# Funnel attention followed by a multiplicative feed-forward: constants through TensorE at the start, another early order, and later key and query transposes on SyncE

## The chip, the cores and the metric

The kernel runs on one core of a Trainium2 chip. The metric is the device time of one execution in microseconds. The kernel before was run three times. A separate execution was profiled; its trace is what is read below. The engines are called as in the profile: PE is TensorE (PEld its weight loads), DVE is VectorE, ACT is ScalarE, POOL is GpSimd, SP is SyncE, which here only issues DMAs.

## What is computed

Eight batches of eight heads, 1152 positions, 64 features a head. Queries are averaged in pairs, which leaves 576 rows a head; after attention, the heads of a batch stand side by side as 512 features of 4608 tokens, which go through two gates, a product, and two more matrices.

```python
def _attn_ref(q, k, v):
    q_pool = q.reshape(B, H, S // 2, 2, D).mean(axis=3)
    scores = scale * np.matmul(q_pool, k.transpose(0, 1, 3, 2))
    scores = scores - np.max(scores, axis=-1, keepdims=True)
    attn = np.exp(scores)
    attn = attn / (np.sum(attn, axis=-1, keepdims=True) + 1e-09)
    return np.matmul(attn, v)

def _moe_ref(x, w1, w2, w3, w_out):
    a = x @ w1
    b = x @ w2
    h = a * b @ w3
    return (h @ w_out)
```

Inputs and output are float32; the kernel works in float16 with float32 sums, and leaves the maximum out of the softmax.

## The kernel before

**Pairs and chunks.** Two heads of one batch form a pair P (0 to 31); head u of the pair uses the partitions 64u to 64u+63 of the transposed keys `kT[P]` and pooled queries `qT[P]`. The transposed scores of a pair are 9 key blocks of 128 by 576 queries, 5184 columns for each head. They are cut, across the pairs, into 324 chunks of 512 columns; a pair is 10.125 chunks. `scores(c)` (matmuls at L287) writes a chunk of both heads into one of two PSUM tiles `psc`, `expo(c)` (L293) takes its exponential on ScalarE into a ring `er`. `attend(P, u)` multiplies the exponentials by the values with a column of ones: 36 matmuls at L305, and for u = 0 18 more at L314 for the last 64 query rows of both heads. `normalize` divides on VectorE (L333, L336, L347), and SyncE transposes the result by DMA into `xT` (L341) or, for the last rows, `xR` (L323).

**Feed-forward.** w3 and w_out are multiplied with each other first: w3 is transposed on TensorE (`w3t`, L458), copied (L449), multiplied by w_out (`pT`, L470) and kept as `T16`. When the four pairs of a batch have ended, `add_batch` queues its gates (`pg`, L506: 256 tokens by w1 and by w2 for each of 8 blocks of 128 and each of two parities h; then VectorE L490 and L498 form `gT`) and its rows (`pp`, L527, stored through SyncE). Every fourth batch brings a second unit for the remainder rows in `xR`, 128 wide. Most of these matmuls contract over 64 partitions, one half of the array each: there is a queue for each half, and products of the two halves lie side by side in time.

**Keys and queries.** For pairs 0 to 8 they are transposed on TensorE (`prep_first`, `prep_rest`; `prep_stage` stages, and `prep_pe` transposes, L255). From pair 9 on `prep_dma` does it: POOL rearranges the keys (`kc`, L159), pools the queries (`qp`, L143) and copies the values (L152); SyncE transposes keys (L160) and queries (L162) by DMA; then POOL reads one element of `kT` (`seen`, L166) and issues the loads of pair P + 5, so those start only when the key transpose has landed.

**The order.** No scheduler orders the instructions. The kernel's own loop writes them out by a planner: two clocks, one for each half of the array, are advanced by booked costs (0.219 for the scores of a chunk, 0.216 for a 512-wide half product, and so on), `due(c)` says when the scores of a chunk may come, `step(h)` takes the next product from the queues `prep` and `ffn` if its data are ready by the clock, `bursts` holds the attends. What comes early is tied to the place of the chunk in pairs: `STAGE` and `PREP` (pairs), `early` (chunk and block of w3), `events` (loads, and `copy_v`). Small VectorE work waits in `jobs`, one a chunk. PSUM has two `psc` tiles and four banks `ff0` to `ff3`, which `spare` hands out; a new tile in a bank has to wait for the old one.

**Queues.** All loads go through POOL in the order written: q and k of pair 0, v of pair 0, k and q of pair 1, the first quarter of w3, w_out whole (`load_w`), then pair 2 and so on. SyncE's queue holds the transposes and the stores in the order written; an entry whose data are not ready holds those behind it.

Of the kernel before, what the change touches and what calls it, by code (L numbers as in the profile page):

```python
# [8 lines left out]
FP16 = mybir.dt.float16  # L9
# [14 lines left out]
def kernel(  # L24
# [20 lines left out]
    NPE = 9  # L45
    T_SC, T_EXP, T_SEM, T_PV, LEAD = 0.219, 1.03, 0.25, (1.65, 1.3), 2.6
    SCALE = 0.5 * float(D) ** -0.5

# [22 lines left out]
    ctx.enter_context(tc.manual_schedule())  # L71

    for vt in vts:
        nc.vector.memset(vt[:, :, :, D:VW], 1.0 / SCL)
# [6 lines left out]
    exp_done = []  # L81
    spare = [(0.0, n) for n in range(4)]

    def vector(n, at):

        nonlocal vec
        vec = max(vec, at + T_SEM) + 0.16 + n / 960
        return vec

    def bank(pre, n, dt=FP32):  # L90
        if n >= 4:
            return psum.tile([128, 2, 512], FP32, tag="psc", bufs=2, name=pre)[:, 0, :]
        return psum.tile([128, 2048 // (4 if dt == FP32 else 2)], dt, tag=f"ff{n}", bufs=1,
                         name=pre)

    def take():
# [30 lines left out]
    def load(P):  # L127


        if P < NP:  # L130
            load_k(P)
            load_q(P)
        if P <= NP:
            load_v(P - 1)
# [16 lines left out]
    def copy_v(P, eng=None):  # L151
        (eng or nc.vector).tensor_copy(out=vts[P % 4][:, :, :, 0:D], in_=vst.pop(P))  # L152

    def prep_dma(P):

        pp, o = P // 2, 64 * (P % 2)
        new_kq(P)
        kc = ab.tile([128, NJ, 2, D], FP16, tag="kc", bufs=2, name="kc")
        nc.gpsimd.tensor_copy(out=kc.rearrange("p j u d -> p u j d"), in_=kst.pop(P))  # L159
        nc.sync.dma_start_transpose(out=kT[P], in_=kc.rearrange("p j u d -> p (j u d)"))  # L160
        pool_q(P, nc.gpsimd)
        nc.sync.dma_start_transpose(  # L162
            out=qT[P], in_=qps[pp][o:o + 64].rearrange("p c u d -> p (c u d)"))
        copy_v(P, nc.gpsimd)
        if P + 5 <= NP:
            nc.gpsimd.tensor_copy(out=seen[:, 0:1], in_=kT[P][0:1, 0, 0:1])  # L166
            load(P + 5)

# [52 lines left out]
    def prep_rest(tb):  # L221
        nc.vector.tensor_copy(out=kcs[0][:, 3:NJ].rearrange("p j u d -> p u j d"),
                              in_=kst[0][:, :, 3:NJ])
        keys(0, tb, range(3, NJ))
        nc.vector.tensor_copy(out=kT[0][:, 3:NJ].rearrange("p j f -> p (j f)"),
                              in_=tb[:, 0:768])
        copy_v(0)
        del kst[0], kcs[0]
# [133 lines left out]

    def load_w(dst, src):
        nc.gpsimd.dma_start(out=dst, in_=src.rearrange("(c p) f -> p c f", p=128))

# [35 lines left out]

    w3T = {}

    class Block:
# [36 lines left out]
    def w3_transpose(c):  # L441

        w3T[c] = ffp.tile([128, NF, 128], FP16, tag="w3T", bufs=4, name="w3T")
        ready = [1e9]
        left = [2]
        landed = 13.0

        def out(t, at, h):
            nc.vector.tensor_copy(out=w3T[c][:, :, 64 * h:64 * h + 64],  # L449
                                  in_=t[:, 0:512].rearrange("p (a f) -> p a f", f=64))  # L450
            done = vector(256, at)
            left[0] -= 1
            if left[0] == 0:
                ready[0] = max(done + T_SEM, landed)
            return done

        def emit(t, s, n, start, stop):
            nc.tensor.transpose(t[:, 64 * n:64 * n + 64],  # L458
                                w3h[c // 2][s, c % 2, 128 * n:128 * n + 128], ident[s, s])
        for h in range(2):  # L460
            add(prep, Block("w3t", NF, (h,), lambda t, at, h=h: out(t, at, h), FP16),
                0.0285, [[0.0]], emit)

        def copy(t, at):
            nc.vector.tensor_copy(out=T16[:, c, :], in_=t)
            del w3T[c]
            return vector(512, at)

        def product(t, s, n, start, stop):
            nc.tensor.matmul(t, w3T[c][s, n, :], wosb[s, n, :], start=start, stop=stop,  # L470
                             skip_group_check=True)
        add(ffn, Block("pT", NF, (0, 1), copy), 0.216, [ready], product)

    def add_unit(n, x, places, ready, final=False):

# [6 lines left out]
        def gate(ft, h):  # L482
            def mul(t, at):
# [8 lines left out]
                if h not in gT:  # L492
                    gT[h] = ffp.tile([128, NF, 256], FP16, tag="g", bufs=4, name="gT")
                g = gT[h][:, ft, 0:n]
# [39 lines left out]

        for h in range(2):
            for ft in range(NF):
                gate(ft, h)
        for h, o, to in places:
            rows(h, o, to)

    def add_batch(b, ready):

        k, o, end = (b // 2) % 2, 256 * (b % 2), b == B - 1
        add_unit(256, lambda s, m: xT[s, m, k, o:o + 256],
                 [(h, 128 * i, [(b, 4 * i + 2 * h), (b, 4 * i + 2 * h + 1)])
                  for h in range(2) for i in range(2)], ready)
        if b % 4 == 3:
            add_unit(128, lambda s, m: xR[s, m // 2, b // 2 - 1:b // 2 + 1, m % 2],
                     [(h, 0, [(b - 3 + h, 8), (b - 1 + h, 8)]) for h in range(2)],
                     ready, final=end)  # L550

# [35 lines left out]
    def last_rows(places, lhsT):  # L587
# [25 lines left out]
        base=0, channel_multiplier=1, pattern=[[-1, 128]])  # L613
    load_v(0)
    load_k(1)
    load_q(1)
    load_w3(0)
    load_w(wosb, moe_w_out)
    load(2)
# [4 lines left out]
    nc.gpsimd.tensor_copy(out=swap[:, 64:128], in_=ident[:, 0:64])  # L624
    staged, prepped = 1, 1
    rest = prep_first()

    def last_chunk(P):
        return -(-(P + 1) * PAIR // CH) - 1

    def copy_v_later(P):
        if P < 4:
            jobs.append((560, lambda: copy_v(P)))
        else:
            copy_v(P, nc.gpsimd)

    early = [(14, 0), (14, 1), (19, 2), (20, 3), (26, 4), (27, 5), (33, 6), (34, 7)]
    STAGE = {1: 0.39, 2: 1.4, 3: 2.15, 4: 2.85, 5: 3.85}
    PREP = {1: 0.55, 2: 1.6, 3: 2.45, 4: 3.2, 5: 4.1}
    events = sorted(  # L640
        [(0.0, 4, load), (0.0, 3, load_w3), (0.4, 5, load), (0.4, 0, load_ffn), (1.2, 6, load),
         (1.2, 1, load_ffn), (2.3, 7, load), (4.0, 8, load), (4.75, 9, load), (5.0, 10, load),
         (5.95, 11, load), (6.95, 12, load), (7.05, 13, load)]
        + list(zip((1.75, 2.6, 3.7, 4.35, 5.1, 5.4, 6.1, 7.0), range(1, NPE),
                   [copy_v_later] * NPE)), key=lambda e: e[0])
    WEIGHTS = (47.0, 57.0)
    jobs = []
    kq_done[0] = 0.0
    bursts = sorted([(last_chunk(P) + (2 if u == 1 else 6), P, u)
                     for P in range(NP) for u in range(2)])  # L650

    def due(c):


        if bursts and (c + 1) * CH > bursts[0][1] * PAIR + RING:
            return 1e9
        P = ((c + 1) * CH - 1) // PAIR
        return max(exp_done[c - 2] if c > 1 else 0.0, kq_done.get(P, 0.0))

    c = 0  # L660
    fresh = False
    while c < NCHUNK or bursts or ffn[0] or ffn[1]:
        h = 0 if clock[0] <= clock[1] else 1
        if bursts and (c > bursts[0][0] or c == NCHUNK) and spare and spare[0][0] < clock[h] and (
                fresh or c > bursts[0][0] + 1 or c == NCHUNK):
            attend(*bursts.pop(0)[1:])
            fresh = False
            while swap_due():
                swap_halves()
            continue  # L670
        if c >= NCHUNK or due(c) > clock[h]:
# [5 lines left out]
            if not step(h):  # L677
                if swap_due():
                    clock[:] = [max(clock) + 0.1] * 2
                    swap_halves()  # L680
                    clock[:] = [clock[0] + 0.1] * 2
                else:
                    clock[h] += 0.02
# [9 lines left out]
        expo(c)  # L693
        exp_done.append(max(exp_done[-1] if c else 0.0, max(clock) + T_SEM) + T_EXP)
        if c == 0:
            prep_rest(rest)
        if jobs:
            n, job = jobs.pop(0)
            job()
            vector(n, 0.0)  # L700
        if staged < NPE and at >= STAGE.get(
                staged, staged - (0.95 if staged < 4 else 1.3)):
            prep_stage(staged)
            staged += 1
        while events and at >= events[0][0]:
            _, n, act = events.pop(0)
            act(n)
        todo = prepped < NP and at >= PREP.get(prepped, prepped - (
            0.65 if prepped < 4 else 0.9 if prepped < NPE else 1.9))
        if todo and prepped >= NPE:  # L710
            prep_dma(prepped)
            prepped += 1
        elif todo and prepped < staged and prepped in kcs:
            prep_pe(prepped)
            prepped += 1
        elif early and c >= early[0][0] and len(w3T) < 4:
            w3_transpose(early.pop(0)[1])
        c += 1
# [37 lines left out]
```

## Time and profile before

| what | value |
|---|---|
| median of 3 runs | 424.46 us (422.82 to 424.8) |
| the profiled execution | 422.81 us |
| its span, first to last instruction | 420.7 us |
| first scores on PE, first exponential on ACT | 8.05 us, 8.70 us |
| last exponential | starts at 367.4 us |
| ACT exponentials (L293) | 324, 308.2 us, 1029 ns each |
| waits of POOL's `seen` for the key transpose | 83.6 us in 19 |
| key transpose, issue to landing (median of 23) | 7.4 us |
| xT transpose, issue to landing (median of 64) | 4.7 us |

Times in the trace count from the first instruction of the program, L12 is line 12 of the kernel before. Group lines read: line, engine, operation, out<-in, shape, count, then busy time and mean ns of one, then the idle time of the engine just before them and what ended it. Busy matmuls overlap, so a busy TensorE need not be at its peak: its two halves may be filled by one product alone. The granted clock (PEclk) is what the throttle allowed, as a share of full speed.

### The profile page before, as it was taken

The page shows a single profiled execution, that of the slowest core. Times are in us where ns is not written, and L with a number is a line of the kernel's source. Part 1 is how long each engine was busy: PE and PEld are TensorE (multiplying, and loading weights), DVE is VectorE, ACT ScalarE, POOL GpSimd, SP SyncE. Part 2 cuts the span into 40 slices and gives each one's busy share as a digit, 9 for nine tenths or more (in the row PEclk, how much of TensorE's full clock was granted, in tenths as well). Part 3 has the DMA queues.
Part 4 walks back from the last instruction along what each step waited for, and adds up shares of the span by engine and source line. Part 5 has one row for each costly group of instructions (what it writes and reads, how often), then busy time and mean ns, then how long its engine had stood idle before and what let it go on. Part 6 is the DMA issues. An engine that isn't in the chain of part 4 may idle for free.

```text
span 420.7 us, 17427 instructions
## 1 busy us (share of the span) xinstructions
PE 402.0 (96%) x7666; PEld 320.2 (76%) x7666; DVE 219.9 (52%) x596; ACT 330.7 (79%) x382; POOL 191.6 (46%) x209
## 2 busy tenths in 40 slices
PE   3799999999999999999999997999999999999996
PEld 1366665678778877888788886888878887888894
DVE  3266656876436654664356455466446644542432
ACT  3968888988888888888788896889888888834342
POOL 8243345762564675665645764556688100000000
PEclk9999999999999999999999999999999999999999
DMA  8999999999999999989999999999997422102021
GB/s 120 204 207 201 186 205 200 180 170 142 141 169 185 161 148 164 184 136 121 156 198 130 150 167 186 145 145 173 119 147 160 52 45 92 44 19 101 2 104 51
DMA packets 94219, 59.02 MB, mean 140 GB/s; under 512 B 64832, under 2 KB 84544, under 8 KB 94144
## 3 DMA queue, kind: packets, MB, share of 16 engines
q0 software_dynamic: 26528, 33.56, 51.8%
q1 hardware_dynamic: 67456, 24.22, 36.5%
q8 instruction: 60, 0.98, 1.0%
q10 hardware_dynamic: 160, 0.13, 0.1%
q14 instruction: 15, 0.12, 0.1%
HBM read 67.11 MB, written 9.44 MB: 182 GB/s over the span
## 4 chain that ended last, share of the span: by engine, by line
PE 92%; ACT 3%; DMA 2%; issue 1%; DVE 0%; POOL 0%; ACTq 0%; POOLq 0%
PE pg L506 30%; PE psc L287 19%; PE po L305 18%; PE pp L527 14%; PE pT L470 4%; PE po L314 3%; ACT er L293 3%; PE t L255 1%; DMA xT<-xn 1%; PE sw L384 1%; DMA kst<-in_k_dram 1%; PE w3t L458 0%; PE pp L593 0%; POOL qst L108 0%; PE tb L188 0%
## 5 line engine op out<-in xcount | busy, mean ns | idle before, releaser
L293 ACT ACTIVATE er<-psc 128x1024 f16<-128x1024 f32 x324 | 308.2, 1029 | 49.8 <-PE psc L287 43.7
L287 PE MATMUL psc<-qT,kT 64*128 64x384 f16 (+7 forms) x1152 | 132.3, 291 | 3.9 <-ACT er L293 3.5
L506 PE MATMUL pg<-xT,w2sb 64*128 64x256 f16 x1024 | 129.3, 269 | 0.0
L506 PE MATMUL pg<-xT,w1sb 64*128 64x256 f16 x1024 | 128.4, 269 | 1.0 <-DMA xT<-xn 0.9
L506 PEld LDWEIGHTS <-w1sb 64*128 64x128 f16 x1280 | 102.0, 94 | 9.9 <-issue 1.6
L506 PEld LDWEIGHTS <-w2sb 64*128 64x128 f16 x1280 | 102.0, 94 | 6.0
L527 PE MATMUL pp<-T,gT 64*128 64x512 f16 (+1 forms) x552 | 98.2, 376 | 0.0
L305 PEld LDWEIGHTS <-er 128*128 128x128 f16 x2304 | 74.6, 98 | 18.4 <-issue 15.3
L305 PE MATMUL po<-vt,er 128*128 128x65 f16 x2304 | 82.5, 194 | 2.8 <-issue 2.5
L287 PEld LDWEIGHTS <-kT 64*128 64x128 f16 x1152 | 60.9, 95 | 30.5 <-issue 15.9
L498 DVE TENSOR_TENSOR gT<-pg,asb 128x256 f16<-128x256 f32 (+1 forms) x160 | 66.2, 416 | 24.1 <-ACT asb L487 19.9
L490 DVE COPY asb<-pg 128x256 f32<-128x256 f32 (+1 forms) x119 | 48.1, 404 | 27.4 <-PE pg L506 25.7
L333 DVE RECIPROCAL rz<-po 128x4 f32<-128x4 f32 x64 | 12.1, 189 | 92.8 <-PE po L305 48.2
L143 POOL TENSOR_TENSOR qp<-qst 64x1152 f16<-64x1152 f16 x23 | 54.4, 2367 | 1.0
L527 PEld LDWEIGHTS <-gT 64*128 64x128 f16 (+1 forms) x552 | 43.0, 94 | 11.1
L166 POOL COPY seen<-kT 1x1 f16<-1x1 f16 x19 | 3.4, 181 | 83.6 <-DMA kT<-kc 83.6
L152 POOL COPY vt<-vst 128x1152 f16<-128x1152 f16 x28 | 32.1, 1149 | 6.6 <-issue 5.4
L123 POOL DMA_DIRECT2D vst<-in_v_dram x32 | 23.2, 725 | 19.1 <-DMA kst<-in_k_dram 7.2
L116 POOL DMA_DIRECT2D kst<-in_k_dram x33 | 24.0, 728 | 11.8 <-DMA kst<-in_k_dram 2.7
L487 ACT COPY asb<-pg 128x256 f32<-128x256 f32 (+1 forms) x41 | 13.1, 331 | 19.7 <-PE pg L506 18.6
L336 DVE TENSOR_TENSOR xn<-po,rz 128x256 f16<-128x256 f32 x64 | 27.2, 424 | 2.2
L159 POOL COPY kc<-kst 128x1152 f16<-128x1152 f16 x23 | 26.8, 1164 | 0.8 <-DMA kT<-kc 0.8
(62 smaller groups left out, 254.2 us busy)
## 6 DMA issues: line engine op xcount, KB each, us to landing
qst<-in_q_dram POOLq DMA_DIRECT2D x32, 288.0 KB, 6.9
vst<-in_v_dram POOLq DMA_DIRECT2D x32, 288.0 KB, 8.3
kst<-in_k_dram POOLq DMA_DIRECT2D x31, 288.0 KB, 6.0
out_dram<-osb SPq DMA_DIRECT2D x32, 256.0 KB, 3.4
w3h<-in_moe_w_dram POOLq DMA_DIRECT2D x4, 512.0 KB, 14.5
wosb<-in_moe_w_out_dram POOLq DMA_DIRECT2D x1, 1024.0 KB, 13.8
xT<-xn SPq DMA_TRANSPOSE x64, 4.7
w1sb<-in_moe_w_dram POOLq DMA_DIRECT2D x2, 512.0 KB, 15.6
```

What stands on the lines that cost most here:

```text
L116: nc.gpsimd.dma_start(out=kst[P][:, :, js[0]:js[1], :], in_=k[b, h0:h0 + 2].rearrange("u (p j) d -> p u j d", j=NJ)[:, :, js[0]:js[1], :])
L143: (eng or nc.vector).tensor_tensor(out=qps[pp][r].rearrange("p c u d -> p u c d"), in0=src[:, :, :, 0, :], in1=src[:, :, :, 1, :], op=ALU.add)
L152: (eng or nc.vector).tensor_copy(out=vts[P % 4][:, :, :, 0:D], in_=vst.pop(P))
L159: nc.gpsimd.tensor_copy(out=kc.rearrange("p j u d -> p u j d"), in_=kst.pop(P))
L287: nc.tensor.matmul(t[:, u, o:o + ln], kT[P][s, j, :], qv[s, f0:f0 + ln], start=True, stop=True)
L293: nc.scalar.activation(out=er[:, :, r:r + CH], in_=psc.pop(c), func=AF.Exp, bias=0.0, scale=SCALE)
L305: nc.tensor.matmul(po[:, VW * i:VW * i + D + 1], er[:, u, r:r + 128], vts[P % 4][:, u, j, 0:D + 1], start=(j == 0 and i == 0), stop=(j == ...
L336: nc.vector.tensor_tensor(out=xn, in0=acc[:, 0:4, 0:D], in1=rz[:, 0:4].to_broadcast([128, 4, D]), op=ALU.mult)
L490: nc.vector.tensor_copy(out=a, in_=t[:, 0:n])
L498: nc.vector.tensor_mul(out=g, in0=b, in1=a)
L506: nc.tensor.matmul(t[:, n * w:n * w + n], (w1sb, w2sb)[w][s, (m + h) % 2, m // 2, fs], x(s, m), start=start, stop=stop, skip_group_check=True)
L527: nc.tensor.matmul(t, gT[h][s, i, cs], T16[s, i, :], start=start, stop=stop, skip_group_check=True)
```

## The change

Four things are changed. (1) *Constants.* A row block of `T16` is set to 0.5; `busy` multiplies it with itself into a bank, `idle`, that nobody reads: 11 times 128x512 before anything else on TensorE, and 45 times 64x256 wherever half 0 of the planner has nothing to do before its clock reaches `BUSY` = 13; bank 3 is kept for that until then. (2) *Early order.* v of pair 0 is loaded after w3 and w_out, w_out in two halves of 256 columns, and the products of w3's first two blocks with w_out are split in the same way (`columns`, each half with its landing time `WOUT`); staging, preparation and w3 blocks are released by `landed`, at planner times (`STAGE`, `W3`) instead of at chunks; the attends of pair 0 come a chunk later; the planner books exponentials 0.11 shorter up to chunk 70. (3) *SyncE.* `prep_dma` leaves the key and query transposes to `turns`, which are emitted at pair P - 1.45 and P - 1.2 instead of about P - 1.9, with `seen` and the loads of pair P + 5 behind the key transpose. (4) *Gates.* In every fourth batch the 128-wide gates are put between the 256-wide ones instead of behind them; their `gT` is cut to width and shares the buffers of `w3T`. The program has 56 fillers more on TensorE and, for the split, 32 products more; of DMAs it has one more.

```diff
+    BUSY = 13.0
+    nc.vector.memset(T16[:, 0, :], 0.5)
-    spare = [(0.0, n) for n in range(4)]
+    spare = [(0.0, n) for n in range(3)] + [(BUSY, 3)]
+    def busy(s, n):
+        nc.tensor.matmul(bank("idle", 3)[:, 0:n], T16[s, 0, 0:128], T16[s, 0, 0:n],
+                         start=True, stop=True)
...
+    turns = []
     def prep_dma(P):
         pp, o = P // 2, 64 * (P % 2)
         new_kq(P)
         kc = ab.tile([128, NJ, 2, D], FP16, tag="kc", bufs=2, name="kc")
         nc.gpsimd.tensor_copy(out=kc.rearrange("p j u d -> p u j d"), in_=kst.pop(P))
-        nc.sync.dma_start_transpose(out=kT[P], in_=kc.rearrange("p j u d -> p (j u d)"))
         pool_q(P, nc.gpsimd)
-        nc.sync.dma_start_transpose(
-            out=qT[P], in_=qps[pp][o:o + 64].rearrange("p c u d -> p (c u d)"))
         copy_v(P, nc.gpsimd)
-        if P + 5 <= NP:
-            nc.gpsimd.tensor_copy(out=seen[:, 0:1], in_=kT[P][0:1, 0, 0:1])
-            load(P + 5)
+        def turn_k():
+            nc.sync.dma_start_transpose(out=kT[P], in_=kc.rearrange("p j u d -> p (j u d)"))
+            if P + 5 <= NP:
+                nc.gpsimd.tensor_copy(out=seen[:, 0:1], in_=kT[P][0:1, 0, 0:1])
+                load(P + 5)
+        def turn_q():
+            nc.sync.dma_start_transpose(
+                out=qT[P], in_=qps[pp][o:o + 64].rearrange("p c u d -> p (c u d)"))
+        turns.extend([(P - 1.45, turn_k), (P - 1.2, turn_q)])
...
-    def load_w(dst, src):
-        nc.gpsimd.dma_start(out=dst, in_=src.rearrange("(c p) f -> p c f", p=128))
+    def load_w_out(cols):
+        nc.gpsimd.dma_start(out=wosb[:, :, cols],
+                            in_=moe_w_out.rearrange("(c p) f -> p c f", p=128)[:, :, cols])
...
+        if c > 1:
+            columns(slice(0, dm), 0.0)
+            return
+        columns(slice(0, 256), WOUT[0])
+        second.append(lambda: columns(slice(256, 512), WOUT[1]))
+        if c == 1:
+            for part in second:
+                part()
...
+        gates = [next(u) for u in units]
+        for h in range(2):
+            order = [(ft, gates[0]) for ft in range(NF)]
+            for ft in range(NF if len(gates) > 1 else 0):
+                order.insert(4 + 3 * ft // 2, (ft, gates[1]))
+            for ft, gate in order:
+                gate(ft, h)
...
-    load_v(0)
     load_k(1)
     load_q(1)
     load_w3(0)
-    load_w(wosb, moe_w_out)
+    for half in range(2):
+        load_w_out(slice(256 * half, 256 * half + 256))
+    load_v(0)
...
+    for _ in range(11):
+        busy(slice(0, 128), 512)
     rest = prep_first()
...
+    def landed(c, before=0.0):
+        nonlocal staged, prepped
+        if vec < max(clock) + 0.3:
+            job()
+        if staged < NPE and max(clock) + before >= STAGE[staged] and kq_done.get(staged - 1, 1e9) < 1e9:
+            prep_stage(staged)
+            staged += 1
+        if prepped < staged:
+            if not jobs:
+                prep_pe(prepped)
+                prepped += 1
+        elif early and max(clock) >= W3[early[0] // 2] and len(w3T) < 4:
+            w3_transpose(early.pop(0))
...
-    early = [(14, 0), (14, 1), (19, 2), (20, 3), (26, 4), (27, 5), (33, 6), (34, 7)]
-    STAGE = {1: 0.39, 2: 1.4, 3: 2.15, 4: 2.85, 5: 3.85}
-    PREP = {1: 0.55, 2: 1.6, 3: 2.45, 4: 3.2, 5: 4.1}
+    EARLY = 70
+    W3 = (5.2, 19.3, 27.2, 35.7)
+    STAGE = {1: 3.3, 2: 15.4, 3: 22.2, 4: 31.4, 5: 39.0, 6: 49.5, 7: 59.9, 8: 65.5}
+    early = list(range(NF))
-    WEIGHTS = (47.0, 57.0)
+    WEIGHTS, WOUT = (47.0, 57.0), (7.5, 10.6)
-    bursts = sorted([(last_chunk(P) + (2 if u == 1 else 6), P, u)
+    bursts = sorted([(last_chunk(P) + (2 if u == 1 else 6) + (P == 0), P, u)
                      for P in range(NP) for u in range(2)])
...
             if not step(h):
-                if swap_due():
+                if h == 0 and clock[0] < BUSY - 0.2:
+                    busy(slice(0, 64), 256)
+                    clock[0] += 0.13
+                elif swap_due():
...
-        exp_done.append(max(exp_done[-1] if c else 0.0, max(clock) + T_SEM) + T_EXP)
+        over = 0.11 if c < EARLY else 0.0
+        exp_done.append(max(exp_done[-1] - over if c else 0.0, max(clock) + T_SEM) + T_EXP)
...
+        while turns and at >= turns[0][0]:
+            turns.pop(0)[1]()
```

## Prediction

> **What bounds the kernel now.** I read the page's table of engines and its chain first, then the busy time in stretches, then the timeline of the start, then the waits of the queues and the chain in order of time.
>
> ```profile
> PE 402.0 (96%) x7666; PEld 320.2 (76%) x7666; DVE 219.9 (52%) x596; ACT 330.7 (79%) x382; POOL 191.6 (46%) x209
> ...
> PE 92%; ACT 3%; DMA 2%; issue 1%; DVE 0%; POOL 0%; ACTq 0%; POOLq 0%
> ```
>
> TensorE (PE) carries 92% of the chain. Its products are the same before and after, so the time can only come from stretches in which it idles, runs slowly or runs half empty. In stretches of 10 us (columns: stretch, then busy time and count of PE, PEld, DVE, ACT, POOL, then granted clock, DMA share, GB/s) the first one after the start-up is the odd one: ScalarE is full and TensorE is not.
>
> ```profile
> 10.00:20.00 10.00, 6.79 (x67) 2.84 (x63) 3.05 (x7) 9.63 (x11) 2.40 (x4) 1.00 1.18 201
> ...
> 30.00:40.00 10.00, 10.00 (x211) 6.91 (x208) 6.70 (x17) 7.93 (x9) 4.37 (x7) 1.00 1.16 205
> ```
>
> The timeline of TensorE (start, length, line, tiles, shape, count) shows what it does there, and that it is slow:
>
> ```profile
> 6.27 0.39 PE L210 MATMUL tq<-ident,qp 64*128 64x64 f16 x4 [6.27 <-DVE qp L204]
> ...
> 8.05 0.61 PE L287 MATMUL psc<-qT,kT 64*128 64x512 f16 x2 [0.41 <-DVE qT L213]
> ...
> 12.90 0.61 PE L287 MATMUL psc<-qT,kT 64*128 64x320 f16 x4 [0.30 <-ACT er L293]
> ...
> 20.33 2.16 PE L305 MATMUL po<-vt,er 128*128 128x65 f16 x36
> ...
> 33.33 1.27 PE L305 MATMUL po<-vt,er 128*128 128x65 f16 x36
> ...
> 34.53 0.39 PE L287 MATMUL psc<-qT,kT 64*128 64x320 f16 x4
> ```
>
> Four score products take 0.61 us at 12.90 and 0.39 us at 34.53; the 36 products of L305 take 2.16 and then 1.27 us. The granted clock is written as 1.00 in both stretches, so that column does not show it. The short times begin at about 23.5 us, some 3.1 us after the first dense burst at 20.33. Until then a chunk costs what ScalarE takes: six exponentials fill 5.61 us from 10.00, 0.935 us each, and TensorE waits 0.3 us for each. So slowness hurts little there (36 products 0.9 us late, some transposes), and the idle time is real.
>
> Two late stalls are the other thing to gain. The chain in order of time has them, and the waits of SP's queue and of POOL name what stands ahead of the first:
>
> ```profile
> 200.91 4.88 DMA xT<-xn
> ...
> 258.36 2.53 issue
> ```
>
> ```profile
> POOL seen L166 <- DMA kT<-kc: 83.6, 19, 8.3
> ...
> SPq L160 <- POOL kc L159: 40.8, 16, 5.2
> ```
>
> In the timeline xn is done at 196.25, but its transpose is issued at 200.91, behind a key transpose (196.97 to 199.0) and a query transpose (199.30); it lands at 205.8, and TensorE has run half empty since 204.07 and stood 0.92 us. At 258.36 TensorE stops inside a burst of L305 for nothing that the profile shows; ahead of it lie 10 us with 252 products in the stretch 250:260 (211 in 30:40), most of them the short 64x128 gate products of the remainder rows.
>
> **The change, part by part.** Durations are of this execution: span 420.7 us, 422.81 us with what lies around it; the median shown, 424.46, is 1.65 above, and I add the sum to the median.
>
> *Fillers at the front.* 11 products of 128x512 come before everything, after a memset of one T16 row block on VectorE (start 0.82; a 128x36 memset takes 0.088 us, a 128x512 f16 copy 0.416, so it ends between 0.9 and 1.25). All write one PSUM bank under a new name each time, and in the built order each waits on TensorE's own semaphore for the one before. No wait of TensorE on itself binds in the trace of before (the nearest is nine products apart). I price one filler as duration plus one hop: 0.385 (L384, 128x512) to 0.61 (the pair at 8.05), plus 0.05 (DVE qT ends 8.00, psc starts 8.05). That is 4.8 to 7.3 us for 11, or, with five at 0.66 until 3.1 us have passed, 3.3 + 6 x 0.435 = 5.9: end at about 7.05. The first transposes were ready at 6.27, so they come 0.8 late, of which some 0.2 return because they then run at full rate: +0.6 (0 to +2.0).
>
> The Trainium skill, TensorE: Matmul & The Clock Gate, section "The HAM clock gate", says that the array runs at half rate until about 3.4 us of sustained activity: by it 5 to 6 fillers run at half rate, an estimate of 7.1 us for their end. The 3.1 us of the trace say almost the same, while the granted clock that the profile prints does not show the half rate at all.
>
> *Fillers between the scores.* 45 products of 64x256 on one half, which the kernel's own planner books at 0.13 us. They too stand in single file. One costs 0.269 (L506, 64x256) + 0.05 = 0.315 at full rate; at half rate 0.40 + 0.05 = 0.45 (between 0.237 for 64 columns at L210 and 0.61 for 512); without the wait 0.109 (16 products of L506 in 0.87, two halves). I take 0.315. Everything behind a waiting filler waits too: the next scores, and ScalarE for them. Counted in the built order between the scores of chunks 1 and 9 (counted from 0): 9, 5, 5, 6, 3 (and 27 transposes), 6, 3 (and 16), 4 (and 8) fillers. The intervals are 2.85, 1.6, 1.6, 1.9, 1.3, 1.9, 1.2, 1.5, sum 13.85 us. The same eight exponentials go from 10.00 to 17.80 in before, 7.80. So the chain of exponentials falls 6.05 us back.
>
> *Early order.* v of pair 0 goes behind w3 and w_out, w_out is loaded in two halves, w3's transposes and the first products of w3 and w_out move ahead of the first burst of L305. Bytes up to w_out and v are the same, so v lands at about 20.5 (POOL's wait on w_out ends at 20.83); with the fillers' delay the burst that needs it comes near 30, so nothing waits; one more issue of 0.7 us on POOL lies in its idle 1.67 us before 12.03. Chunks 9 to 18: by the order 9.85 us (two bursts, now at full rate: 1.20 and 1.60; 57 half-width products; the last 4 fillers) against 10.65 in before (17.80 to 28.45): -0.8. By then 57 x 0.054 = 3.1 us of w3-w_out products are done against 8 x 0.108 = 0.86: 2.25 us of later work is out of the way. Net of fillers and order: 6.05 - 0.8 - 2.25 = +3.0 (bounds -3.0 without the waits, +8.3 at half rate). VectorE gets four 256-wide copies for two 512-wide and two 0.14 us handovers; it is 52% busy: 0. Until 60 us the two orders then do the same work with waits of the same kind: 0 (-2, if being late hides landings, to +1).
>
> *Transposes later on SyncE.* 23 key and 23 query transposes are issued about 0.45 and 0.7 of a pair (a pair is some 10.9 us) later, no DMA is added. Each key transpose is now placed where its copy should be done, so the 40.8 us that SP's queue waits for POOL shrink, and xT, queued behind, goes earlier. POOL's copy `seen` and the next loads move with the key transpose. Gain: the stall at 204 to 206, 0.92 standing and 1.1 half empty, and some smaller: -1.5 (-2.9 to +2). What it costs without that cover is the third rival.
>
> *Gates of the remainder rows interleaved.* No product is added; 64x128 products alternate with 64x256 ones, so fewer instructions a microsecond. If density made the stall at 258.36, it goes: -2.5 (-2.7 to 0).
>
> Sum: 0.6 + 3.0 + 0 - 1.5 - 2.5 = -0.4; 424.46 - 0.4 = 424.1.
>
> **The rivals.**
> 1. *The fillers don't hold each other up* (the wait on the own semaphore is met early): 9 fillers cost 1.0 us, which fits into ScalarE's 0.935 a chunk. Then 6.05 and 0.6 vanish: -0.4 - 6.65 = -7.0, 417.5. For it: 0.13 us a filler is a plan that would work at 0.109. Against: VectorE starts 0.04 us after the modelled end of the product it waits for (tq ends 7.64, copy at 7.68), so a semaphore comes with the end, not with the start.
> 2. *The fillers leave the array at half rate*, on the slower side. Scores alone, 0.61 of each 0.92 us, did not make it fast in before; fillers with a hop between them may not either. Then a filler is 0.45, the eight intervals sum to 19.1, and the front ends at 8.4: +5.25 + 1.3, 430.7. It decides as soon as the 64x256 filler stays at 0.40. Against: one is in flight nine tenths of the time, more than the scores were. The Trainium skill, TensorE: Matmul & The Clock Gate, section "A second HAM failure mode", tells of micro-idles between products that drop the clock again; no run here shows it yet.
> 3. *The late gains don't come*: POOL's loop is key transpose (median 7.4 us to landing), seen, three loads (2.3), next copy (1.16), some 11.1 us, against 10.9 a pair. With the transpose later, its slack of about 8 us is used up by pair 25 or so; xT still waits behind it, and the instruction stall stays. -4.0 is lost: 428.1.
>
> **How the numbers follow.** Forecast 0.47 (own range 421 to 427), fillers overlapping 0.23, array at half rate 0.17, no late gains 0.13. Under 0.5%, 2.1 us, a measurement of this kernel tells nothing from no change. Faster: all of the second, a fifth of the first: 0.34. Same: three fifths of the first and a little of the last: 0.30. Slower: the rest, 0.36. The range is 417.5 to 430.5, from the overlapping fillers to the array at half rate.
>
> **What would show it.** Starts of neighbouring 64x256 fillers 0.31 us apart (0.11 for the first rival, 0.45 for the second); exponential 2, counted from 0, at about 13.3 instead of 10.94, and exponential 18 near 34; first scores at 8.6; psc of a chunk at 0.39 instead of 0.61 from the start; no stall in L305 after the remainder gates; xT issued within 2 us of xn up to pair 15. I am wrong if exponentials 2 to 9 still come every 0.93 us, or if new waits of scores for kT appear after pair 20.

## The result, and the profile after

The changed kernel takes 440.18 us (median of 4 runs, 438.53 to 440.8), the kernel before 424.63 beside it (422.82 to 425.27, 4 runs): ratio 1.0368, 95% interval 1.0322 to 1.0413. It is 15.6 us slower; the forecast was 424.1, the range ended at 430.5. The profiled execution has a span of 437.9 us, 17.2 more than before's 420.7. Medians and ranges here and below are over all executions, while a ratio and its interval leave out those more than 1.5% above the fastest of their kernel, so a ratio is not the quotient of the medians.

The table of engines and the chain on the page of the changed kernel:

```profile
PE 423.7 (97%) x7754; PEld 326.0 (74%) x7754; DVE 219.9 (50%) x598; ACT 332.6 (76%) x385; POOL 192.6 (44%) x210
...
PE 95%; issue 2%; ACT 2%; DVE 0%; ACTq 0%; DVEq 0%
```

TensorE is busy 21.7 us longer, for 88 instructions more: 56 fillers and 32 half-width products. ScalarE's and VectorE's work is what it was. Where the time lies is seen in the stretches of 10 us at the start (columns as in the prediction):

```profile
10.00:20.00 10.00, 9.07 (x40) 3.53 (x41) 2.01 (x4) 4.09 (x4) 3.25 (x5) 1.00 1.31 199
20.00:30.00 10.00, 9.41 (x97) 5.60 (x94) 2.55 (x6) 4.41 (x5) 4.01 (x8) 1.00 1.16 208
30.00:40.00 10.00, 9.77 (x72) 5.92 (x70) 1.98 (x7) 5.49 (x6) 4.69 (x7) 1.00 1.15 209
```

ScalarE, 9.63 us busy from 10 to 20 in before, has 4.09 now, and TensorE has what looks like more work. Its timeline at the start says what that work is:

```profile
1.47 7.01 PE L101 MATMUL idle<-T 128*128 128x512 f16 x11 [1.47 <-DVE T L74]
...
10.03 0.61 PE L301 MATMUL psc<-qT,kT 64*128 64x512 f16 x2 [0.42 <-DVE qT L228]
...
11.72 3.82 PE L101 MATMUL idle<-T 64*128 64x256 f16 x9
15.18 0.79 PE L301 MATMUL psc<-qT,kT 64*128 64x128 f16 x4
15.77 2.12 PE L101 MATMUL idle<-T 64*128 64x256 f16 x5
```

Eleven fillers take 7.01 us, one every 0.64; the first scores come at 10.03 instead of 8.05. Nine of the half-array fillers take 3.82, one every 0.43, and the scores of a chunk, behind them in the same queue, wait. Products stay at the long durations until 39 us (before: until 24).

The difference over the run, from the starts of the exponentials (counted from 0) in both traces (differences are of the unrounded times):

| stretch | before, us | after, us | difference |
|---|---|---|---|
| start to exponential 1 | 10.00 | 11.97 | +2.0 |
| 1 to 9 | 7.80 | 20.05 | +12.3 |
| 9 to 18 | 10.65 | 13.76 | +3.1 |
| 18 to 45 | 30.34 | 28.36 | -2.0 |
| 45 to 323 | 308.6 | 307.4 | -1.1 |
| last exponential to the end | 53.3 | 56.4 | +3.0 |

Late in the run, the wait of 4.88 us for xT, in before at 200.91, is gone from the chain, but the stall with no visible cause is now two. From the chain in order of time, and from the waits of GpSimd and of SyncE's queue:

```profile
256.15 1.31 issue
...
267.76 0.99 issue
```

```profile
POOL seen L176 <- DMA kT<-kc: 89.8, 19, 10.8
...
SPq L174 <- POOL kc L169: 29.8, 11, 4.7
```

SyncE's queue waits 29.8 us for GpSimd's key copies instead of 40.8; GpSimd waits a little longer for the transposes (89.8 for 83.6).

### The profile page after: what moved, and what is told of

Read it like the earlier page. It is cut to its first block, busy times and chain, and to the rows that moved or that the text cites. A ratio compares the mean times of both kernels' runs of the same rounds, so it can differ in the third digit from the quotient of the medians.

```text
span 437.9 us, 17616 instructions
## 1 busy us (share of the span) xinstructions
PE 423.7 (97%) x7754; PEld 326.0 (74%) x7754; DVE 219.9 (50%) x598; ACT 332.6 (76%) x385; POOL 192.6 (44%) x210
## 4 chain that ended last, share of the span: by engine, by line
PE 95%; issue 2%; ACT 2%; DVE 0%; ACTq 0%; DVEq 0%
PE pg L534 29%; PE psc L301 19%; PE po L319 17%; PE pp L555 14%; PE idle L101 5%; PE pT L489 4%; PE po L328 3%; ACT er L307 2%; PE sw L399 1%; PE t L269 1%; PE w3t L473 1%; PE pp L628 0%; PE tb L203 0%; PE tq L225 0%; DVE T L74 0%
## 5 line engine op out<-in xcount | busy, mean ns | idle before, releaser
L301 PE MATMUL psc<-qT,kT 64*128 64x192 f16 (+7 forms) x1152 | 133.8, 291 | 4.4 <-issue 2.0
L534 PEld LDWEIGHTS <-w1sb 64*128 64x128 f16 x1280 | 96.3, 94 | 7.8 <-issue 0.5
L534 PEld LDWEIGHTS <-w2sb 64*128 64x128 f16 x1280 | 95.4, 94 | 6.4 <-issue 0.2
L555 PE MATMUL pp<-T,gT 64*128 64x512 f16 (+1 forms) x552 | 94.7, 376 | 0.0
L301 PEld LDWEIGHTS <-kT 64*128 64x128 f16 x1152 | 62.2, 95 | 31.6 <-issue 16.1
L517 DVE COPY asb<-pg 128x256 f32<-128x256 f32 (+1 forms) x116 | 46.8, 403 | 28.6 <-PE pg L534 27.0
L555 PEld LDWEIGHTS <-gT 64*128 64x128 f16 (+1 forms) x552 | 39.8, 94 | 15.1 <-issue 0.4
L176 POOL COPY seen<-kT 1x1 f16<-1x1 f16 x19 | 3.4, 179 | 89.8 <-DMA kT<-kc 89.8
L489 PE MATMUL pT<-wosb,w3T 64*128 64x512 f16 (+1 forms) x160 | 29.2, 369 | 0.2 <-DVE kT L263 0.2
L116 POOL DMA_DIRECT2D qst<-in_q_dram x32 | 19.7, 615 | 19.7 <-DVE qp L151 8.7
```

Of the source, the lines that this page charges most:

```text
L301: nc.tensor.matmul(t[:, u, o:o + ln], kT[P][s, j, :], qv[s, f0:f0 + ln], start=True, stop=True)
L489: nc.tensor.matmul(t[:, 0:m], w3T[c][s, n, :], wosb[s, n, cols], start=start, stop=stop, skip_group_check=True)
L517: nc.vector.tensor_copy(out=a, in_=t[:, 0:n])
L534: nc.tensor.matmul(t[:, n * w:n * w + n], (w1sb, w2sb)[w][s, (m + h) % 2, m // 2, fs], x(s, m), start=start, stop=stop, skip_group_check=True)
L555: nc.tensor.matmul(t, gT[h][s, i, cs], T16[s, i, :], start=start, stop=stop, skip_group_check=True)
```

## The experiments

Each is the changed kernel with the edit shown (the first seven), or the kernel before with parts of the change or with the copies moved (the rest). Diffs are shortened. "Before" is the kernel before, run on the same chip.

### Take the fillers apart

**No filler.** All 56 are out; the planner still books their 0.13.

```diff
     def busy(s, n):
-        nc.tensor.matmul(bank("idle", 3)[:, 0:n], ...)
+        pass
```

> The changed kernel with all 56 fillers left out, every other instruction and its order kept (the planner still books them). Theory S (the fillers stand in single file at 0.42 us each and hold the scores back): the 17.1 us by which exponential 12 came later go, exponential 12 at about 20 us, and the rest of the change is left with its own effect, -1 to -5 us on before: 420 to 424. Theory O (the early order itself is what costs, products of w3 and w_out at half rate ahead of the scores): 432 or more, exponential 12 still after 28 us.

Measured: 424.03 (before 424.89), ratio 0.9964 (0.9918 to 1.001). The fillers are the loss; what else the change does is worth some -1.5 us by the ratio, not clear of nothing.

**The 11 at the front only**, and **the 45 between the scores only**, each with the other call taken out:

```diff
-                    busy(slice(0, 64), 256)
```
```diff
-    for _ in range(11):
-        busy(slice(0, 128), 512)
```

> The changed kernel with the 11 fillers at the front and without the 45 between the scores. Theory S: 2 us later at the first scores (10.0 instead of 8.05), nothing after that: e1 plus 1 to 2.5 us. If the front leaves the array at full rate for the scores (psc pairs of 0.39 us), e1 plus 0 or less. Theory O: as e1.

> The changed kernel with the 45 fillers between the scores and without the 11 at the front. Theory S: 13 to 16 us over e1, about 438; fillers 0.42 us apart and at half rate. If the rate is what matters and the front made it worse or better, clearly off 438.

Measured: front only 424.92, ratio 1.0015 (0.9973 to 1.0057); middle only 436.15, ratio 1.0274 (1.0193 to 1.0354). Over the kernel without fillers, by the ratios, the front costs 2.2 us (the two intervals overlap), the middle 13.2, both 17.2; the 1.8 by which the whole exceeds its parts are not explained. In the trace of the front alone the first scores are 2.0 late; with the middle alone they come on time, at 8.04, and the fillers behind them stand 0.42 to 0.48 apart.

**All 56 into one tile.** The tile is taken once, so no filler has to wait for the one before; number, size and place stay.

```diff
+    idle = []
     def busy(s, n):
-        nc.tensor.matmul(bank("idle", 3)[:, 0:n], ...)
+        if not idle:
+            idle.append(bank("idle", 3))
+        nc.tensor.matmul(idle[0][:, 0:n], ...)
```

> All 56 fillers, but all written into one PSUM tile that is taken once, so none waits for the one before. Theory S, wait as the cause: fillers 0.21 us apart at half rate or 0.11 at full rate, the front ends near 6.2 us, the chain of exponentials at most 4 us behind e1; if they also bring the full rate early, e1 or 1 to 2 us below it: 418 to 424. If the half rate alone is the cause and the wait is nothing: spacing 0.21, but still 6 us or more over e1: 428 and up.

Measured: 425.11, ratio 1.0007 (0.9961 to 1.0053). The 15 us are gone with the waits alone. Its timeline of TensorE:

```profile
1.46 4.87 PE L103 MATMUL idle<-T 128*128 128x512 f16 x11 [1.46 <-DVE T L74]
...
7.83 0.39 PE L303 MATMUL psc<-qT,kT 64*128 64x512 f16 x2 [0.41 <-DVE qT L230]
...
8.82 0.81 PE L103 MATMUL idle<-T 64*128 64x256 f16 x6
```

Eleven fillers take 4.87 instead of 7.01, and the first scores run at 0.39 at once. The half-array fillers stand 0.11 apart ((0.81 - 0.27) / 5). But the early full rate brings nothing to the whole that is clear of noise: ScalarE sets the pace there, with exponentials 1 to 9 0.92 us apart. The edit took the waits and the half rate away together; what each costs by itself it does not say.

**Front in one tile, middle waiting.** The wait and the rate fell together so far; here the array is at full rate before the first waiting filler.

```diff
+    idle = bank("idle", 3)
     for _ in range(11):
-        busy(slice(0, 128), 512)
+        nc.tensor.matmul(idle, T16[:, 0, 0:128], T16[:, 0, :], start=True, stop=True)
```

> The 11 fillers of the front are written into one tile taken once, so nothing holds them up; the 45 between the scores wait for each other as in the changed kernel. This separates the wait from the rate, which fell together there. If the rate that the array has reached holds through waiting fillers: full rate from about 7 us, first scores at 7.8, neighbouring 64x256 fillers 0.31 us apart (0.269 and one hop), exponential 9 near 23.5, exponential 18 about 5 us behind before, the whole 427 to 429. If fillers with a gap between them bring the array back to half rate: 0.42 apart, exponential 9 near 29, exponential 18 some 13 behind, the whole 434 to 437, as with the middle fillers alone (436.15).

Measured: 436.84, ratio 1.0314 (1.0247 to 1.038), as the second expectation has it. Its timeline of TensorE in two short windows, and its stretches (the third number from the end is the granted clock):

```profile
8.99 1.56 PE L101 MATMUL idle<-T 64*128 64x256 f16 x5
...
12.48 1.70 PE L101 MATMUL idle<-T 64*128 64x256 f16 x4
```

```profile
8.00:10.00 2.00, 1.83 (x16) 0.88 (x16) 0.77 (x2) 1.57 (x2) 2.00 (x4) 1.00 1.06 173
10.00:12.00 2.00, 1.72 (x8) 0.57 (x8) 0.36 (x1) 0.36 (x1) 0.61 (x2) 0.61 1.05 179
12.00:14.00 2.00, 1.83 (x9) 0.72 (x7) 0.85 (x2) 1.02 (x1) 0.62 (x1) 0.50 1.30 196
...
32.00:34.00 2.00, 1.94 (x18) 1.23 (x14) 0.52 (x2) 1.02 (x1) 0.71 (x1) 0.50 1.14 205
34.00:36.00 2.00, 2.00 (x33) 1.57 (x28) 0.95 (x3) 1.64 (x2) 0.77 (x1) 0.92 1.16 211
```

The first five fillers stand 0.32 us apart ((1.56 - 0.27) / 4), the price of the prediction. That lasts 1.4 us: at 10.4 the granted clock falls to 0.50, the next stand 0.43 apart ((1.70 - 0.41) / 3), and it stays there until 34.3, while 41 of the 45 are issued by 27.9. Waiting fillers do not hold the rate up, and the scores between them do not either. So the run did not part the two: apart from those 1.4 us, hardly a waiting filler in any run is at full rate. It also shows what the column leaves out: this drop is printed, while the half rate from the first instruction on, in before and after, stands as 1.00. The column knows a change, not the first state; the durations do.

**Front in one tile, no middle.** The edit of the last run, and besides:

```diff
-                    busy(slice(0, 64), 256)
```

> The 11 fillers of the front in one tile, none between the scores; the rest of the change stays. If the array keeps the full rate that it reaches by about 7 us: first scores at 7.8, exponential 9 at 16.6 or earlier (before 17.8, without any filler 17.5), exponential 18 near 26.5 (28.45, 27.4). If an early lead is lost again at 74 to 80 us, as without any filler: chunk 72 no more than 1 us ahead and the whole 423 to 425. If it reaches the end: 421 to 422.

Measured: 424.21 (before 424.67), ratio 0.9987 (0.9947 to 1.0027). First scores early and at full rate, exponential 9 at 17.2 and not 16.6: the granted clock is 0.50 from 9.6 to 16.4, so scores at ScalarE's pace did not hold it either:

```profile
10.00:11.00 1.00, 0.61 (x4) 0.28 (x4) 0.00 (x0) 1.00 (x2) 0.67 (x1) 0.50 1.10 182
```

The fall at 10.4 in the run before can't be put down to the waiting fillers, then; that the rate came back only at 34.3 there, and at 16.4 here, is what goes with them. This execution was 3.7 us ahead of before's at chunk 72, 5.4 at the last exponential and 2.4 at its end; the median of 12 is not ahead: one profile is one execution, of a kernel whose times spread over 7 us.

### Where the early gain of the rest goes

Without fillers the kernel is 3.1 us ahead at chunk 63 and level at chunk 72. VectorE, GpSimd and TensorE at that place of the run without fillers:

```profile
73.93 4.45 DVE L148 TENSOR_TENSOR qp<-qst 64x1152 f16<-64x1152 f16 x1
```
```profile
74.44 2.24 POOL L157 COPY vt<-vst 128x1152 f16<-128x1152 f16 x2
76.61 1.15 POOL L190 COPY kc<-kst 128x1152 f16<-128x1152 f16 x1
```
```profile
79.46 0.19 PE L266 MATMUL t<-ident,kc 64*128 64x64 f16 x1 [2.23 <-DVE rz L344]
```

The pooling of queries takes 4.45 us; the eight of that size in before take 0.74 to 0.76. It ends at 78.38, 0.6 us after GpSimd's last copy: it seems to stand while they run. What is queued behind it on VectorE is late, TensorE waits 2.23 us for that from 77.22, and from 81.1 to 84.5 its granted clock is 0.50. The Trainium skill, SBUF — State Buffer, section "Who interferes with whom", says that a VectorE instruction with two inputs in SBUF contends with a GpSimd instruction that reads SBUF. The trace agrees, with 4.45 for 0.75. The same section of the Trainium skill says that whoever issues first gets the shared ports; here the pooling, which starts 0.5 us before the copies by the profile, is the one held up.

**The copies on VectorE.** As the run with the front in one tile and no middle, and values of pairs 4 to 8 and keys of pairs 7 and 8 copied on VectorE:

```diff
-        if P < 7:
-            jobs.append((280, copy_k))
-        else:
-            copy_k(nc.gpsimd)
-            kc_done[P] = max(clock) + 3.0
+        jobs.append((280, copy_k))
...
-        if P < 4:
-            jobs.append((560, lambda: copy_v(P)))
-        else:
-            copy_v(P, nc.gpsimd)
+        jobs.append((560, lambda: copy_v(P)))
```

> As the run with dense front fillers alone, and besides the copies of the values of pairs 4 to 8 and of the keys of pairs 7 and 8 are made on VectorE instead of GpSimd. If GpSimd's copies beside it are what stretched VectorE's pooling of queries from 0.75 to 4.45 us: all poolings before 88 us take 0.75, no gap of TensorE over 1 us at 74 to 80 us, chunk 72 2.5 to 3 us ahead of before, and the whole 1 to 3 us under its companion, 421 to 423. If the pooling was long for another reason: it is long again, and the whole stays at 423 to 425. VectorE gets 7 copies of some 0.45 us more; if one of them waits for a load, products behind it are late and it is above the companion.

Measured: 423.41, ratio 0.9971 (0.9937 to 1.0005). Every pooling of that size takes 0.73 to 0.76 now, and no gap over 0.5 us is left at 74 to 80 us; the mechanism is as supposed. But its companion met the collision only in part (1.80 us at 74.60), and the times of the two are not told apart.

### The other parts, one by one, on the kernel before

**Transposes later.** `turns` as in the change, nothing else.

```diff
-        nc.sync.dma_start_transpose(out=kT[P], ...)
...
+        turns.extend([(P - 1.45, turn_k), (P - 1.2, turn_q)])
...
+        while turns and at >= turns[0][0]:
+            turns.pop(0)[1]()
```

> The kernel before with one part of the change, the key and query transposes later on SyncE. By the prediction: the stall of TensorE at 204 to 206 us goes, the waits of SP's queue for GpSimd's key copy shrink from 40.8 us, -1.5, 423.4. By the rival: GpSimd's waits for the key transpose grow past 83.6 us, loads and new waits of scores for kT come late in the loop, 425 to 428. What the run without fillers showed at chunk 180 (1.4 us gained there) speaks for the first.

Measured: 421.35 (419.51 to 424.64, 10 runs; before 425.07), ratio 0.9926 (0.9881 to 0.9972): better than the changed kernel, and better than before by an interval that leaves out 1. In its trace the stall behind xT is gone, and the exponentials gain 1.2 us at chunk 178; SyncE's waits for the key copy are 26.5 us. GpSimd's wait for the transposes grows to 89.6; no wait of scores for keys comes of it. The profiled execution hid the gain, since its pooling met GpSimd's copies:

```profile
76.79 2.95 DVE L143 TENSOR_TENSOR qp<-qst 64x1152 f16<-64x1152 f16 x1
```
```profile
76.87 1.16 POOL L152 COPY vt<-vst 128x1152 f16<-128x1152 f16 x1
77.96 1.15 POOL L185 COPY kc<-kst 128x1152 f16<-128x1152 f16 x1
```

In before the same pooling starts at 76.22 and is done 0.42 us ahead of the copy at 77.40.

**Gates between each other.** `unit` and `add_batch` as in the change, nothing else.

```diff
-        for h in range(2):
-            for ft in range(NF):
-                gate(ft, h)
+        yield gate
...
+                order.insert(4 + 3 * ft // 2, (ft, gates[1]))
```

> The kernel before with one part of the change, the gates of the remainder rows between the others. By the prediction the stall of 2.53 us at 258 us, for nothing that the profile shows, goes with the dense stretch ahead of it: -2.5, 422.4. If such stalls only move, as the changed kernel's at 256 and 268 us suggest: stalls of 0.5 us or more of the same kind stay between 240 and 290 us, with 1.5 to 3 us in all, and the whole is 424 to 425.5.

Measured: 424.19 (before 425.07), ratio 1.0008 (0.9971 to 1.0044). From its chain in order of time:

```profile
201.97 4.79 DMA xT<-xn
...
239.47 1.80 issue
```

The wait for xT is still there, and the stall of 258 stands at 239, with one of 0.62 at 251.67. The interleaving moved the stall and did not remove it. Stalls of this kind, 0.8 to 2.5 us, lie between 229 and 273 us in most traces (none in the three with fillers at the front and none between the scores), and elsewhere too (1.37 at 106.93 and 1.60 at 196.31 with the front alone).

The traces show what TensorE waits for there: its own instructions. The page of before has a DMA queue for them:

```profile
q8 instruction: 60, 0.98, 1.0%
```

These are 60 packets of 16 KB, one for each 256 of TensorE's 15,332 matmuls and weight loads. In the 14 traces 35 gaps of TensorE of 0.5 us or more, between 45 and 370 us, end with nothing that the profile shows as their cause. Counted in matmuls and weight loads, all 35 stand 179 to 192 above a multiple of 256, and each ends 1.2 to 1.7 us after such a packet has landed: before's stall, which ends at 260.90, after one that started at 258.16 and landed at 259.34. That also fits a stall that moves with the order. Why the packet starts so late at some of these places, and whether short products that use up 256 instructions sooner have a part in it, stays open.

**Transposes later, and the copies on VectorE**: the diff of the transposes and that of the copies above, together.

> The kernel before with the transposes later on SyncE, and with the copies of the values of pairs 4 to 8 and the keys of pairs 7 and 8 on VectorE instead of GpSimd. In the run with the transposes alone VectorE's pooling at 76.79 us took 2.95 us beside two copies of GpSimd and TensorE then stood 1.58 us. If those copies hold it up: every pooling takes 0.75, no gap of TensorE over 1 us at 76 to 82 us, chunk 72 within 0.7 us of before, and the whole is 1 to 2 us under the transposes alone: 419.5 to 420.5, ratio 0.988 to 0.990. If the collision is rare over executions, it stays at 421.4. If VectorE's longer queue costs more than it saves: 422 to 424.

Measured: 422.28 (before 424.95), ratio 0.9958 (0.9918 to 0.9999). The pooling is short again:

```profile
76.95 0.76 DVE L143 TENSOR_TENSOR qp<-qst 64x1152 f16<-64x1152 f16 x1
```

and there is no gap there, yet the whole is not under the transposes alone. The profile shows a cost of the cure: GpSimd's loads of keys wait 10.3 us for VectorE's copies, which free their buffers.

**The copies alone**: that diff on the kernel before.

> The kernel before with those copies on VectorE alone. In the profile of before the pooling at 76.22 us ends 0.42 us ahead of GpSimd's copy at 77.40, so an execution that lies a little otherwise meets it. If that happens in part of the executions: 0.5 to 2 us gained over all, 423 to 424.5, and no mean clock of 0.992 to 0.996, which goes with before's times of 427 to 433. If before hardly ever meets it: 424.9 or, with VectorE's longer queue, up to 426.

Measured: 424.50 (423.49 to 427.22; before 424.95, 422.42 to 430.48), ratio 0.9997 (0.9965 to 1.0029). No time over 427.22 came in its 12 executions (5 of 23 in before), the median is not lower to speak of, and mean clocks of 0.996 still come. Whether the collision is what spreads before's times is not settled.

**The early order alone**: loads, halves of w_out, releases by time; no filler, transposes and gates as before. Against the run without fillers:

```diff
-        turns.extend([(P - 1.45, turn_k), (P - 1.2, turn_q)])
+        nc.sync.dma_start_transpose(out=kT[P], ...)
...
-                order.insert(4 + 3 * ft // 2, (ft, gates[1]))
```

> The kernel before with the early order alone (loads, halves of w_out, releases by time, pair 0 later); no filler, the transposes on SyncE and the gates as before. Without fillers the whole change had 424.03, ratio 0.9964, and the transposes alone have 0.9926. If the order costs what the two differ by: about +1.5, 426 to 427. If the order gains by its 2.5 to 3 us up to chunk 63 and the rest is scatter: 422 to 424. The place to look: exponentials 36 and 63 2.5 to 3 us ahead, chunk 72 again level if a pooling of queries at about 74 us is long.

Measured: 432.77 (429.81 to 434.75, 6 runs; before 424.95), ratio 1.0179 (1.0127 to 1.0232), worse than either expectation. It is 2.0 us ahead up to chunk 144 and 6.7 behind at 153. TensorE, VectorE and SyncE's queue there:

```profile
180.10 0.37 PE L523 MATMUL pg<-xT,w1sb 64*128 64x256 f16 x1 [6.46 <-DVE osb L537]
```
```profile
179.36 0.69 DVE L537 TENSOR_SCALAR osb<-pp 128x512 f32<-128x512 f32 x1 [9.01 <-DMA out_dram<-osb]
```
```profile
162.81 2.17 SPq L165 DMA_TRANSPOSE kT<-kc  x1
165.24 1.28 SPq L167 DMA_TRANSPOSE qT<-qp  x1
166.62 3.26 SPq L345 DMA_TRANSPOSE xT<-xn  x2
169.97 2.21 SPq L327 DMA_TRANSPOSE xR<-rems  x1
172.27 1.89 SPq L602 DMA_DIRECT2D out_dram<-osb  x3
```

VectorE fills `osb`, of which there are three, at 161.76, 163.76 and 165.92. The first store is issued at 172.27: key, query, xT and xR transposes stand ahead of it on SyncE. The fourth `osb` waits 9.01 us for that store, and with it VectorE's queue, and TensorE 6.46 us. With transposes and gates as in the change (the run without fillers) no such gap is in the trace. So part 3 of the change pays for a wait that part 2 makes; parts priced one by one, on the trace of before, do not show it. That it is the transposes and not the gates is read from the queue; the two were not tried apart under the new order.

## Why the prediction was wrong

*The step that failed* is the rate of the array, and with it the price of a filler. The mechanism was seen: fillers in single file, each held by the one before, scores behind them late. The 0.315 us (0.269 and a hop of 0.05) is right for full rate, 0.32 where the array had it; but I held the array to be at full rate by then, and it was not. Measured: 0.42, and 0.48 for the first of a group, at half rate until 39 us: 11 waiting fillers did not bring the full rate. Exponentials 1 to 9 took 20.05 us, not 13.85. With 41 fillers in the eight intervals the price makes some 4.5 us of the 6.2 (41 x 0.11). The rest is a term that the intervals put at nothing, the scores of the chunk: the nine fillers from 11.72 and the four products behind them take 4.05 us until the next filler at 15.77, some 0.2 more than 9 x 0.425; eight times that is the other 1.7.

Nor did the rows of before show 3.1 us until full rate: their transposes of w3 take 0.63 us for 16 at 23.26 and 0.41 at 24.48, and the scores at 24.15 still 0.50, so the short times begin near 24.2, about 4 us after the burst began. The argument against the second rival, that one filler is in flight nine tenths of the time, took the duration in the trace for work. Dense fillers of 512 columns follow each other in (4.87 - 0.63) / 10 = 0.42 us, which is what one occupies; waiting, they come every 0.64, so by estimate the array streams 66% of the time, and 50% for the 256-wide (half of 0.42, every 0.42). The first did not bring full rate in 7 us, the second did not keep it; without gaps it came 3.4 to 5.7 us after the first filler (in the four runs with a dense front, by the durations).

The Trainium skill, TensorE: Matmul & The Clock Gate, section "The HAM clock gate", gives about 3.4 us of sustained activity; the dense runs agree roughly, and the waiting fillers show that "sustained" was the word to weigh: they were issued for 7 us and did not count as such. The Trainium skill, TensorE: Matmul & The Clock Gate, section "A second HAM failure mode", tells of micro-idles of TensorE when a kernel cycles through PSUM banks; this case is near it, with one bank and a new tile each time, though here the clock does not oscillate but stays low.

By the two traces the change is 17.6 us away from the sum. The rate and the price hold 11.5 of it (1.4 at the front, 6.2 in exponentials 1 to 9, 3.9 from 9 to 18), the late gains 2.9 and the end 3.0; 0.2 is left.

*The fillers at the front*: forecast +0.6, first scores 2.0 late, the upper bound; of the whole 2.2 by the ratios, not clear of nothing.

*The first rival*, fillers that do not hold each other up, fell with the same rows; only one tile for all makes it so.

*Chunks 9 to 18*: forecast 9.85 us at full rate, measured 13.76. The second rival had this wrong too. It gave 19.1 us for exponentials 1 to 9, against 20.05, and was right in kind; it ended at 430.7 because it let the array be fast from chunk 9 on (3.9 us), kept the -4.0 of the late gains and had nothing for the end (3.0).

*Work ahead*, -2.25: -2.0 came by chunk 45, close to what was worked out.

*Transposes on SyncE*, -1.5: alone -3.1 by the ratio (interval -5.0 to -1.2), with the stall that I named gone; the third rival's lost slack did not come. Together with the copies on VectorE, which alone change nothing, they are -1.8 (-3.5 to 0), so the forecast size may well be right. The size in the change cannot be read off, as the order alone needs this part.

*Gates*, -2.5: nothing. The stall is a wait for instructions, which the interleaving moved; whether density has a part in it is not shown.

*Until the end*: the sum has no term for what comes after the last exponential. It took 3.0 us more (56.4 us for 53.3), and every kernel with the new order shows it (the run without fillers 56.4, the order alone 55.9). The traces say why: behind the start of the last exponential stand 433 gate products of 64x256 instead of 379 (427 with the order alone), and the 54 more at the prediction's 0.054 us are 2.9 us, by estimate. So part of what the order gains ahead of the last exponential is work left for after it, and from exponential 45 to the end the change is 1.9 us slower, not 4.0 faster.

## What to carry to other kernels

Warm-up products brought the full rate early here only where they followed each other without a gap. Write them all into one PSUM tile: a new tile each time made each wait for the last, which went with 0.42 us a filler instead of 0.11 and with half rate for everything else until 39 us instead of 24. A filler stands in the same queue as the work, so price it by its spacing, at the rate that the array will have then, and compare the stage with what paces it: here ScalarE did, and early full rate on TensorE was worth nothing clear of noise. Look behind the last product of the stage, too: what an order gains early may be work that it leaves for the end. Before moving entries of one queue, list what stands behind them and how many buffers it frees; a store issued some 10 us after its data on SyncE stopped TensorE two engines away.

## What the hardware showed that was not expected

The granted clock in the trace begins as 1.00 and prints only later drops: 0.50 from 10.4 to 34.3 us in the run with a dense front and a waiting middle, while the same half rate from the start stood as 1.00. A gap of 2.23 us on TensorE, with thin work around it, was followed by 3.4 us at 0.50, beginning 1.6 us after its end; chunks 63 to 72 took 13.1 us there instead of 10.0, so the stall may have cost more than its gap. A VectorE addition of two SBUF operands took 4.45 us instead of 0.75 beside three GpSimd copies in a row, and 2.95 beside two. TensorE also waits for its own instructions: 35 stalls of 0.5 to 2.5 us in 14 traces, for which the profile names no cause, lie at nearly one place of every 256 instructions and end 1.2 to 1.7 us after a 16 KB packet of its instruction queue.
